# VectorE fills the transposes' source itself, the last tiles' routing goes ahead of other work, and half steps alternate with query transposes

## The chip, the core and the metric

The kernel runs on one core of a Trainium2 chip, in one launch. The metric is the device time of a whole execution in microseconds; of several runs the median counts. TensorE (PE) does matmuls and 128x128 transposes into PSUM, ScalarE (ACT) and VectorE (DVE) read PSUM and SBUF, GpSimd (POOL) works on SBUF and issues the indirect DMAs, and SyncE (SP) issues the other DMAs from one queue. Every engine runs its own instructions strictly in the order in which the program wrote them; between engines there are semaphores.

## The reference, cut to what matters

Linear attention with random features, followed by a top-1 mixture of experts with a capacity. B = 4, H = 8, S = 576, D = 64, M = 128 features; N = 2304 rows of width 512; E = 8 experts, F = 1024, capacity 576.

```
phi(x) = exp(x@omega.T - |x|^2/2 - max) / sqrt(m)
kv  = einsum('bhsm,bhsd->bhmd', phi(k), v);  z = sum_s phi(k)
attn = (phi(q) @ kv) / (phi(q) @ z + 1e-6)
x = attn as rows (2304, 512)
expert = argmax(x @ w_gate);  gate = softmax value of that expert
slot  = rank of the row among the rows of its expert (dropped from 576 on)
out[row] = gate * relu(x[row] @ w1[expert]) @ w2[expert]
```

## The kernel before

**Slots of the first part.** The outer loop (`for n in range(NS + LATE)`) runs over slots. A key slot takes four units of 128 keys (batch, group of four heads, ninth of the sequence); a query slot takes a tile of 128 rows. The order is: the keys of batches 0 and 1, query tiles 0 to 4, the keys of batches 2 and 3 (slots 15 to 23), query tiles 5 to 17, and three slots that only drain. In slot n TensorE gets, in this order: `project` of n into the `pj` banks; `numer` of the query tile of n - 3, or `kv_acc` of the key units of n - 2 or n - 3, into `sums`; the transposes `qtr` of the exponentials of slot n - 2 (`transposed`, two banks, each copied out by ScalarE into `qpT`). VectorE takes the maxima of `pj` and the normalisation of a tile, ScalarE the exponentials.

**Tasks.** Work that belongs to no slot stands in generators (`tasks`); `step()` takes each of them one `yield` further, some six or seven times a slot. How many `yield`s lie between two of its instructions decides at which place of each engine's order an instruction is written. Three tasks matter here. `kv_out` runs when the keys of a batch and group are summed: VectorE copies the sums from PSUM to `kv_sb`, POOL copies the kv part of `kv_sb` to `kvc`, and for the second group TensorE transposes `kvc` (`ktr`), VectorE copies that to `kvT`, and TensorE multiplies it with the gate weights (`ksm`). `first_item` loads the first expert's weights through SP and splits them on POOL (`w1hi`, `w1lo`, `w2hi`). `route(a, z)` finds expert, rank and table slot of tiles a to z - 1 (`GROUPS`: 0-4, 5-12, 13-17) on VectorE, with one matmul pair `posr` for the ranks, and POOL scatters the rows' numbers into the table `tab_d`, one indirect DMA a tile. After the first group, POOL gathers the first block rows `xg` of item 0 (`first_rows`), which must wait for SP's load of the list `idx` from the table.

**Row transposes and half steps.** An item is up to 576 rows of one expert, in five blocks. `transpose_x` transposes the gathered rows of a block (`xtri`) into a bank; ScalarE rounds them to `xhi`, VectorE subtracts to `xlo`. A half step (`mm1`) is 12 matmuls, h = relu(x w1) for 128 features and half of the rows; ScalarE writes `hhi` (and `hf`), VectorE `hlo`. Item 0's row transposes and 11 of its 16 half steps are put into query slots by the tables `ROWS_AT` and `HALVES_AT`. In the first part `qtr`, `ktr`, `ksm`, `posr`, `xtri` and the half steps share one ring of two PSUM banks (`bank(..)`, tag "tr"): the third user waits until the first one's bank has been read out. In the item part transposes still share two banks, half steps have four and `mm2` has two.

**Items.** After the slots, item 0 does its last five half steps; between them the rest of the routing tasks is stepped (nine steps after each half step), then `items_list` computes the remaining items into `res`. SP reads `res`, loads the next item's `idx` and weights (`prefetch`), POOL gathers its rows (`gather(1)`). TensorE does `mm2_rest` (16 matmuls) and four tiles `mm2` of 24 matmuls; behind some of them, by `tr_at`, stand the row transposes of item 1. After each tile ScalarE scales the result (`ysi`), then splits a quarter of the next w1 (`w1hi`), then takes the `xhi` of the transposes. Items 1 and 2 run the same way without the first part's remains.

## Time and profile before

| | |
|---|---|
| three runs, median (lowest to highest) | 327.15 us (327.11 to 327.22) |
| the profiled execution | 325.47 us, of which 323.7 us from the first to the last instruction |
| busy in the span | PE 286.3 us (88%), DVE 152.1 (47%), ACT 158.9 (49%), POOL 79.3 (25%) |
| mean granted TensorE clock | 0.951 of full speed |
| chain that ended last | PE 46%, issue 30%, POOL 10%, DMA 7% of the span |

The profiled execution is 1.8 us longer than its span; the runs without a profile lie 1.7 us above it. PE is near its full time in most stretches, so what counts is where it stands idle, which engine or transfer it waits for there, and how long its clock stays at half speed afterwards.

### The profile page before, as it was taken

To read this page: it belongs to the slowest core of one execution; us is meant where nothing else is said; L and a number is where in the kernel's file an instruction comes from. 1 tells how busy PE (TensorE), PEld (TensorE's weight loads), DVE (VectorE), ACT (ScalarE), POOL (GpSimd) and SP (SyncE) were. 2 spreads that over 40 slices of the span, in tenths; PEclk is the share of its full clock that TensorE was granted. 3 is DMA by queue.
4 is the path that set the end of the run, shared out by engine and by line. 5 is a ranking of instruction groups with operands and counts; after the bars stand their busy time and mean duration, and the time that the engine had idled before them with its cause. 6 is when DMAs were issued, how large, how long until landed. Compare 5 with 4: busy or idle time off the path is not lost.

```text
span 323.7 us, 7462 instructions
## 1 busy us (share of the span) xinstructions
PE 286.3 (88%) x2957; PEld 243.9 (75%) x2957; DVE 152.1 (47%) x349; ACT 158.9 (49%) x458; POOL 79.3 (25%) x92
## 2 busy tenths in 40 slices
PE   6999999949999999998789359999999999999950
PEld 5889788839787888888728248899688799958840
DVE  2666688923665764453970132354342234523220
ACT  4896799752788856542202313544352254352410
POOL 1000029497400000000376361160021135011110
PEclk9999999985999999999959959999999999999995
DMA  7987589505567541301000794291071049045020
GB/s 253 409 278 275 221 285 369 206 3 173 207 226 229 174 156 55 141 34 67 0 2 1 233 370 177 40 339 64 26 251 65 34 143 289 9 99 213 32 72 4
DMA packets 30096, 50.38 MB, mean 156 GB/s; under 512 B 5747, under 2 KB 15091, under 8 KB 30036
## 3 DMA queue, kind: packets, MB, share of 16 engines
q1 hardware_dynamic: 26212, 40.80, 37.0%
q0 software_dynamic: 3152, 8.28, 7.5%
q10 hardware_dynamic: 688, 0.73, 0.8%
q8 instruction: 25, 0.41, 0.5%
q14 instruction: 19, 0.16, 0.2%
HBM read 36.80 MB, written 13.28 MB: 155 GB/s over the span
## 4 chain that ended last, share of the span: by engine, by line
PE 46%; issue 30%; POOL 10%; DMA 7%; DVE 2%; ACT 1%; SPq 1%; POOLq 0%
PE hi L328 5%; PE yi L653 5%; PE hi L330 5%; PE yi L655 5%; PE yi L654 5%; PE hi L329 5%; PE pj L135 4%; PE sums L202 4%; POOL tab_d L104 4%; POOL w1lo L123 3%; PE yi L663 2%; DMA xg<-x_d,idx 2%; PE xtri L312 2%; DMA kraw<-kT 2%; POOL w1hi L120 1%
## 5 line engine op out<-in xcount | busy, mean ns | idle before, releaser
L148 ACT ACTIVATE ex<-pj,mx 128x128 f32<-128x128 f32 x288 | 79.1, 397 | 18.9 <-PE sums L202 10.3
L143 DVE TENSOR_REDUCE mx<-pj 128x4 f32<-128x512 f32 (+1 forms) x74 | 46.3, 670 | 24.0 <-PE pj L135 12.8
L328 PE MATMUL hi<-xhi,w1hi 128*128 128x288 f32 x148 | 44.0, 298 | 1.0 <-DVE hloi L336 1.0
L330 PE MATMUL hi<-xlo,w1hi 128*128 128x288 f32 x148 | 43.8, 296 | 0.0
L329 PE MATMUL hi<-xhi,w1lo 128*128 128x288 f32 x148 | 43.6, 294 | 0.0
L653 PE MATMUL yi<-w2hi,hhii 128*128 128x512 f32 x96 | 39.1, 407 | 0.0
L104 POOL DMA_INDIRECT tab_d<-pay,slot x18 | 19.2, 1065 | 78.2 <-DVE slot L390 73.7
L654 PE MATMUL yi<-w2hi,hloi 128*128 128x512 f32 x96 | 37.9, 395 | 0.0
L655 PE MATMUL yi<-w2lo,hhii 128*128 128x512 f32 x96 | 37.8, 394 | 0.0
L316 DVE TENSOR_TENSOR xlo<-xtri,xhi 128x512 fp32r<-128x512 f32 (+1 forms) x20 | 12.7, 638 | 53.2 <-ACT xhi L315 53.2
L104 POOL DMA_INDIRECT out<-ysi,idx x15 | 14.7, 981 | 86.9 <-ACT ysi L680 76.0
L333 ACT ACTIVATE hhii<-hi 128x224 fp32r<-128x224 f32 (+1 forms) x37 | 14.2, 383 | 35.9 <-PE hi L330 34.8
L680 ACT ACTIVATE ysi<-yi,idx 128x512 f32<-128x512 f32 x12 | 8.2, 687 | 43.3 <-issue 34.0
L336 DVE SCALAR_TENSOR_TENSOR hloi<-hi,hhii 128x224 fp32r<-128x224 f32 (+1 forms) x37 | 15.6, 423 | 28.8 <-ACT hfi L335 20.6
L328 PEld LDWEIGHTS hi<-xhi,w1hi 128*128 128x128 f32 x148 | 27.8, 188 | 1.5 <-DVE hloi L336 1.2
L446 ACT COPY qpT<-qtr 128x512 f32<-128x512 f32 x36 | 19.7, 588 | 17.6 <-PE qtr L445 17.1
L330 PEld LDWEIGHTS hi<-xlo,w1hi 128*128 128x128 f32 x148 | 27.8, 188 | 0.2 <-DVE xlo L316 0.2
L329 PEld LDWEIGHTS hi<-xhi,w1lo 128*128 128x128 f32 x148 | 27.8, 188 | 0.0
L300 POOL DMA_INDIRECT xg<-x_d,idx x20 | 21.8, 1091 | 21.2 <-DMA idx<-tab_d 16.6
L135 PE MATMUL pj<-om_sb,kraw 64*128 64x128 f32 x288 | 23.5, 290 | 2.6 <-DMA kraw<-kT 1.6
L202 PE MATMUL sums<-v,ex 128*64 128x65 f32 (+1 forms) x576 | 23.6, 236 | 0.0
L135 PEld LDWEIGHTS pj<-om_sb,kraw 64*128 64x128 f32 x288 | 19.3, 191 | 5.6 <-ACT ex L148 3.6
(107 smaller groups left out, 472.7 us busy)
## 6 DMA issues: line engine op xcount, KB each, us to landing
w1raw<-w SPq DMA_DIRECT2D x16, 512.0 KB, 5.7
w2raw<-w SPq DMA_DIRECT2D x16, 512.0 KB, 6.0
qraw<-qT SPq DMA_DIRECT2D x18, 256.0 KB, 4.6
x_d<-xr SPq DMA_DIRECT2D x18, 256.0 KB, 2.3
out<-zero_sb SPq DMA_DIRECT2D x6, 768.0 KB, 5.6
v<-va SPq DMA_DIRECT2D x7, 650.0 KB, 7.8
kraw<-kT SPq DMA_DIRECT2D x7, 576.0 KB, 6.2
v<-va ACTq DMA_DIRECT2D x1, 390.0 KB, 6.8
```

The source lines that it names most:

```text
L104: ins = nc.gpsimd.indirect_dma_start(out=dst, out_offset=bass.IndirectOffsetOnAxis(ap=index, axis=0), in_=src, in_offset=None, bounds_chec ...
L135: nc.tensor.matmul(pj[i][:, s * M : (s + 1) * M], raw[r, :], om_sb[r, :], start=True, stop=True, skip_group_check=True)
L143: nc.vector.tensor_reduce(mx[:, i, 0 : pj[i].shape[1]], pj[i], op=ALU.max, axis=AX.X, negate=True)
L148: nc.scalar.activation(ex[:, i, s, :], pj[i][:, s, :], AF.Exp, bias=mx[:, i, s : s + 1], scale=1.0)
L202: nc.tensor.matmul(acc[c : c + 64, i * 2 * VW + o : i * 2 * VW + o + (z - a) * VW], ex[:, i, c : c + 64], v[:, i, a * VW : z * VW], start= ...
L300: nc.gpsimd.indirect_dma_start(out=big["xg"][0:n, i, :], out_offset=None, in_=x_d[0:rows, :], in_offset=bass.IndirectOffsetOnAxis(ap=big[" ...
L328: nc.tensor.matmul(pt, whi_[:, k, fs], xhi[:, k, sl], start=(k == 0), stop=False)
L329: nc.tensor.matmul(pt, wlo_[:, k, fs], xhi[:, k, sl], start=False, stop=False)
L330: nc.tensor.matmul(pt, whi_[:, k, fs], xlo[:, k, sl], start=False, stop=(k == 3))
L653: nc.tensor.matmul(pt, hhi[:, f, sl], w2hi, start=(f == 0), stop=False)
L654: nc.tensor.matmul(pt, hlo[:, f, sl], w2hi, start=False, stop=False)
L655: nc.tensor.matmul(pt, hhi[:, f, sl], w2lo, start=False, stop=(f == 7))
```

## The change

VectorE, not POOL, fills `kvc`, straight from PSUM and directly behind its copy to `kv_sb`; the two pauses between go away. `route` has single yields everywhere, and the sum and reciprocal of the softmax stand behind the slots instead of ahead of the ranks. The last group's routing is no longer a task: at the start of the item part all tasks are run out, the group's VectorE part is written, then two half steps, then its ranks, slots, scatters and the whole `items_list`, then the other three half steps. The splits of w2 (`w2lo`) go behind the half steps, and the first `mm2` tile does its products with `w2lo` last. For item 0, SP issues the next w1 loads ahead of the list `idx`. In a query slot one row transpose or half step is written between the two banks of query transposes; the row transposes are one a slot from tile 8 on, and the half steps are single up to tile 17 and double in the three draining slots. Item 1's row transposes stand three behind the third tile and two behind the fourth, instead of two, two and one behind the second to fourth.

```diff
-ROWS_AT = {10: (0,), 11: (1, 2), 12: (3, 4)}
-HALVES_AT = {13: 1, 14: 1, 15: 2, 16: 2, 17: 2, 18: 1, 19: 1, 20: 1}
+ROWS_AT = {t: (t - 8,) for t in range(8, 13)}
+HALVES_AT = {13: 1, 14: 1, 15: 1, 16: 1, 17: 1, 18: 2, 19: 2, 20: 2}
...
         nc.vector.tensor_copy(kv[:, :, 0:VW], acc[:, 0 : 4 * VW].rearrange("p (h c) -> p h c", h=4))
-        yield from pause(2)
-        nc.gpsimd.tensor_copy(kvc[:, g * 2 * M : (g + 1) * 2 * M].rearrange("p (h c) -> p h c", h=4), kv[:, :, 0:D])
+        src = acc[:, 0 : 4 * VW].rearrange("p (h c) -> p h c", h=4)[:, :, 0:D]
+        nc.vector.tensor_copy(kvc[:, g * 2 * M : (g + 1) * 2 * M].rearrange("p (h c) -> p h c", h=4), src)
...
-        gap = 3 if 0 < a and z < NT else 1
...
-            yield from pause(gap)
+            yield
             nc.vector.tensor_tensor(cum[:, t + 1, :], cum[:, t, :], oh[:, t, :], op=ALU.add)
-        yield from pause(gap)
-        nc.vector.tensor_reduce(sm, ex, op=ALU.add, axis=AX.X)
...
-        yield from pause(gap)
+        yield "tensor"
         pos = bank(f"pos{nm}")[:, 0 : T * E]
...
         nc.vector.scalar_tensor_tensor(slot[:, a:z], drop, float(E * REG), base, op0=ALU.add, op1=ALU.add)
+        yield
+        nc.vector.tensor_reduce(sm, ex, op=ALU.add, axis=AX.X)
+        yield
+        nc.vector.tensor_scalar(sm, sm, 1e-9, None, op0=ALU.add)
+        yield
+        nc.vector.reciprocal(pay[:, a:z, 1].bitcast(F32), sm)
...
-        return qpT
+            yield qpT
...
-            if three[1] in GROUPS:
+            if three[1] in GROUPS and three[1] < NT - 1:
                 tasks.append(route(*GROUPS[three[1]]))
         step()
-        if two[0] == "q":
-            qpT_l[n - 2] = transposed(ex_l.pop(n - 2), f"{n - 2}")
...
+        tr = transposed(ex_l.pop(n - 2), f"{n - 2}") if two[0] == "q" else iter(())
+        qpT_l[n - 2] = next(tr, None)
+        if extra:
+            extra.pop(0)()
+        next(tr, None)
...
             if kind:
                 exponent(ex, pj, mx, i)
-            if i < len(extra):
-                extra[i]()
             step(2)
+        for x in extra:
+            x()
...
-    def mm2(i, pt, hhi, hlo):
+    def mm2(i, pt, hhi, hlo, lo_last):
...
+        if lo_last:
+            prods.sort(key=lambda x: x[1] is lo)
...
-                load_idx(sv, j + 1)
+                if j > 0:
+                    load_idx(sv, j + 1)
                 for c in range(4):
                     load_w(1, c, ev)
+                if j == 0:
+                    load_idx(sv, j + 1)
...
+                for _ in chain(*tasks):
+                    pass
+                ro = route(*GROUPS[NT - 1])
+                while next(ro) != "tensor":
+                    pass
                 for n, (f, half) in enumerate(halves):
                     mm1(f, half, bank(f"h{nm}{f}{half}", "h", 4), hhi, hlo, hf)
-                    if n < 4:
-                        split_w_lo(2, n)
-                    for _ in range(9):
-                        next(il, 0)
-                for _ in il:
-                    pass
+                    if n == 1:
+                        for _ in chain(ro, items_list()):
+                            pass
+                for c in range(4):
+                    split_w_lo(2, c)
...
-            tr_at = {2: (0, 1), 3: (2, 3), 4: (4,)} if j == 0 else {i: (i,) for i in range(NSUB)}
+            tr_at = {3: (0, 1, 2), 4: (3, 4)} if j == 0 else {i: (i,) for i in range(NSUB)}
```

Three places show how instructions move. The first is TensorE in the second round of keys, where the second group of batch 2 is complete; `sums` of `v_533` and `v_619` (before) or `v_625` (changed) are the last of its key sums, `ktr` and `ksm` its kv transposes and gate product. Before:

```order
L202 MATMUL sums<-v_533,ex_1077 64x65 x8
L202 MATMUL sums<-v_619,ex_1077 64x65 x8
L135 MATMUL pj_1245<-om_sb,kraw_822 128x128
...
L202 MATMUL sums<-v_619,ex_1126 64x65 x8
L202 MATMUL sums<-v_619,ex_1126 64x130 x4
L202 MATMUL sums<-v_619,ex_1126 64x65 x4
L225 MATMUL ktr_1276<-id_sb,kvc 128x128 x4
L231 MATMUL ksm_1292<-wg_sb,kvT 64x16 x8
```

Changed:

```order
L202 MATMUL sums<-v_533,ex_1077 64x65 x8
L202 MATMUL sums<-v_625,ex_1077 64x65 x8
L225 MATMUL ktr_1245<-id_sb,kvc 128x128 x4
L135 MATMUL pj_1251<-om_sb,kraw_822 128x128
...
L202 MATMUL sums<-v_625,ex_1131 64x65 x8
L202 MATMUL sums<-v_625,ex_1131 64x130 x4
L202 MATMUL sums<-v_625,ex_1131 64x65 x4
L231 MATMUL ksm_1288<-wg_sb,kvT 64x16 x8
```

The kv transposes stand a slot earlier, directly behind the sums they depend on, and a whole slot lies between them and the gate product.

The second place is VectorE around the last group's routing (`mxr` to `pay`; `hloi` belongs to half steps, `w2lo` to the split of w2, `ilcnt` is the first of `items_list`). Before, from the slots of the second group on:

```order
L390 SCALAR_TENSOR_TENSOR slot<-or_2010,br_2009 128x8
L336 SCALAR_TENSOR_TENSOR hloi_1453<-hi_2470,hhii_1452 128x224
L123 TENSOR_TENSOR w2lo_2418<-w2raw_108,w2hi_112 128x1024
L336 SCALAR_TENSOR_TENSOR hloi_1453<-hi_2499,hhii_1452 128x288
L123 TENSOR_TENSOR w2lo_2419<-w2raw_109,w2hi_113 128x1024
L336 SCALAR_TENSOR_TENSOR hloi_1453<-hi_2527,hhii_1452 128x224
L358 TENSOR_REDUCE mxr_2386<-lg 128x5
...
L390 SCALAR_TENSOR_TENSOR slot<-or_2393,br_2392 128x5
L589 TENSOR_SCALAR ilcnt<-cps,cap_f 1x16
```

Changed:

```order
L336 SCALAR_TENSOR_TENSOR hloi_1459<-h_2421,hhii_1458 128x288
L357 TENSOR_REDUCE mxr_2452<-lg 128x5
...
L371 TENSOR_TENSOR cum<-cum,oh 128x8 x5
L336 SCALAR_TENSOR_TENSOR hloi_1459<-hi_2472,hhii_1458 128x224
L336 SCALAR_TENSOR_TENSOR hloi_1459<-hi_2488,hhii_1458 128x288
L376 TENSOR_TENSOR sr_2456<-posr_2503,oh 128x40
...
L383 SCALAR_TENSOR_TENSOR slot<-or_2459,br_2458 128x5
...
L389 RECIPROCAL pay<-mr_2460 128x5
L591 TENSOR_SCALAR ilcnt<-cps,cap_f 1x16
```

The routing of tiles 13 to 17 stood behind all five half steps and two of the shown splits; now it stands behind the last half step of the slots (`h_2421`) and is done behind two of the five.

The third place is TensorE at item 1's row transposes (`xtri`), between item 0's tiles (`yi`). Before, behind the second tile, and the same again behind the third:

```order
L655 MATMUL yi_2699<-w2lo_2419,hhii_1452 128x512
L312 MATMUL xtri_2730<-id_sb,xg 128x128 x4
L312 MATMUL xtri_2737<-id_sb,xg 128x128 x4
L653 MATMUL yi_2745<-w2hi_110,hhii_1452 128x512
L654 MATMUL yi_2745<-w2hi_110,hloi_1453 128x512
```

Changed, behind the third tile:

```order
L660 MATMUL yi_2731<-w2lo_2443,hhii_1458 128x512
L312 MATMUL xtri_2762<-id_sb,xg 128x128 x4
L312 MATMUL xtri_2769<-id_sb,xg 128x128 x4
L312 MATMUL xtri_2776<-id_sb,xg 128x128 x4
L660 MATMUL yi_2784<-w2hi_110,hhii_1458 128x512
L660 MATMUL yi_2784<-w2hi_110,hloi_1459 128x512
```

Three blocks now follow one another on the two transpose banks.

## Rows read from the trace of the kernel before

**Rows 1.** What PE waited for, whole run: total us, times, longest.

```profile
PE xtri L312 <- DMA xg<-x_d,idx: 8.3, 2, 8.1
PE ktr L225 <- POOL kvc L219: 3.6, 1, 3.6
PE posr L381 <- DVE oh L369: 2.8, 1, 2.8
PE h L328 <- ACT qpT L446: 1.8, 6, 0.3
PE ksm L231 <- DVE kvT L226: 1.6, 2, 0.8
...
PE qtr L445 <- ACT qpT L446: 1.4, 2, 0.7
...
PE hi L328 <- DVE hloi L336: 1.0, 1, 1.0
...
PE xtri L312 <- ACT qpT L446: 0.8, 3, 0.3
PE posr L382 <- DVE cum L372: 0.6, 1, 0.6
```

**Rows 2.** Stretches: length, busy PE, PEld, DVE, ACT, POOL, clock, DMA share, GB/s.

```profile
72.00:76.00 4.00, 3.22 (x35) 2.81 (x36) 0.91 (x2) 0.00 (x0) 3.13 (x5) 0.50 0.29 61
76.00:80.00 4.00, 4.00 (x50) 3.66 (x52) 1.72 (x3) 2.04 (x8) 3.10 (x4) 0.50 0.62 195
...
162.00:162.50 0.50, 0.06 (x1) 0.05 (x1) 0.43 (x3) 0.00 (x0) 0.26 (x1) 0.50 0.00 0
```

**Rows 3.** Timeline of PE, second round of keys: start, us, instruction.

```profile
54.92 1.36 PE L202 MATMUL sums<-v,ex 128*64 128x130 f32 x32
...
62.85 1.15 PE L202 MATMUL sums<-v,ex 128*64 128x65 f32 x32
```

**Rows 4.** Timeline of DVE, the same stretch.

```profile
57.58 0.74 DVE L372 TENSOR_TENSOR cum<-cum,oh 128x8 bf16<-128x8 bf16 x4
...
64.40 0.41 DVE L217 COPY kv_sb<-sums 128x260 f32<-128x260 f32 x1
```

**Rows 5.** Timeline of PE from the end of item 0's half steps on.

```profile
163.56 6.25 PE L663 MATMUL yi<-w2raw,hfi 128*64 128x512 f32 x16
...
189.16 1.09 PE L312 MATMUL xtri<-id_sb,xg 128*128 128x128 f32 x4 [8.05 <-DMA xg<-x_d,idx]
...
197.56 1.04 PE L312 MATMUL xtri<-id_sb,xg 128*128 128x128 f32 x8
```

**Rows 6.** The chain that ended last, 173 to 190 us and 230 us: start, us, what.

```profile
173.80 0.98 POOL tab_d L104
...
175.08 3.02 DMA tab_d<-pay,slot
...
178.11 3.50 DMA idx<-tab_d
...
183.74 6.64 DMA xg<-x_d,idx
...
230.34 0.13 PE hi L330
230.47 3.58 PE yi L663 x16
...
234.88 0.23 PE yi L654
```

**Rows 7.** Timeline of DVE in the item part: routing of tiles 13-17, and item 1's `xlo`.

```profile
161.28 0.18 DVE L358 TENSOR_REDUCE mxr<-lg 128x5 f32<-128x40 f32 x1
...
164.64 0.17 DVE L390 SCALAR_TENSOR_TENSOR slot<-or,br 128x5 int32<-128x5 f32 x1
...
199.95 1.29 DVE L316 TENSOR_TENSOR xlo<-xtri,xhi 128x512 fp32r<-128x512 f32 x2 [5.87 <-ACT xhi L315]
```

More of the change, by code (lines that the diff above doesn't have):

```diff
@@ L365, in route @@
         nc.scalar.activation(ex, d, AF.Exp)
-        yield from pause(gap)
+        yield
         nc.vector.tensor_reduce(vm[:, a:z], val, op=ALU.max, axis=AX.X)
-        yield from pause(gap)
+        yield
         nc.vector.tensor_tensor(oh[:, a:z, :], val, vm[:, a:z].unsqueeze(2).to_broadcast(t3), op=ALU.is_equal)
         for t in range(a, z):
-            yield from pause(gap)
+            yield
             nc.vector.tensor_tensor(cum[:, t + 1, :], cum[:, t, :], oh[:, t, :], op=ALU.add)
-        yield from pause(gap)
-        nc.vector.tensor_reduce(sm, ex, op=ALU.add, axis=AX.X)
-        yield from pause(gap)
-        nc.vector.tensor_scalar(sm, sm, 1e-9, None, op0=ALU.add)
-        yield from pause(gap)
-        nc.vector.reciprocal(pay[:, a:z, 1].bitcast(F32), sm)
-        yield from pause(gap)
+        yield "tensor"
         pos = bank(f"pos{nm}")[:, 0 : T * E]
@@ L390, in route @@
         nc.vector.scalar_tensor_tensor(slot[:, a:z], drop, float(E * REG), base, op0=ALU.add, op1=ALU.add)
+        yield
+        nc.vector.tensor_reduce(sm, ex, op=ALU.add, axis=AX.X)
+        yield
+        nc.vector.tensor_scalar(sm, sm, 1e-9, None, op0=ALU.add)
+        yield
+        nc.vector.reciprocal(pay[:, a:z, 1].bitcast(F32), sm)
         yield from pause(2)
@@ L480, in step @@
         for _ in range(n):
-            tasks[:] = [x for x in tasks if next(x, 0) is None]
+            tasks[:] = [x for x in tasks if next(x, 0) != 0]
     def key_groups(b0, first):
@@ L648, in attention_moe @@
     res = const.tile([1, 2, 16], I32, name="res")
-    def mm2(i, pt, hhi, hlo):
+    def mm2(i, pt, hhi, hlo, lo_last):
         sl = slice(i * SUB, (i + 1) * SUB)
-        for f in range(8):
-            w2hi, w2lo = w_hi[2][f // 2][:, f % 2, :], w_lo[2][f // 2][:, f % 2, :]
-            nc.tensor.matmul(pt, hhi[:, f, sl], w2hi, start=(f == 0), stop=False)
-            nc.tensor.matmul(pt, hlo[:, f, sl], w2hi, start=False, stop=False)
-            nc.tensor.matmul(pt, hhi[:, f, sl], w2lo, start=False, stop=(f == 7))
+        hi = [w_hi[2][f // 2][:, f % 2, :] for f in range(8)]
+        lo = [w_lo[2][f // 2][:, f % 2, :] for f in range(8)]
+        prods = [((hhi, hi, f), (hlo, hi, f), (hhi, lo, f)) for f in range(8)]
+        prods = [x for p in prods for x in p]
+        if lo_last:
+            prods.sort(key=lambda x: x[1] is lo)
+        for n, (h, w, f) in enumerate(prods):
+            nc.tensor.matmul(pt, h[:, f, sl], w[f], start=(n == 0), stop=(n == len(prods) - 1))
     def mm2_rest(pt, hf):
@@ L691, in attention_moe @@
             hhi, hlo, hf = h_sb if j == 0 else h_tiles(nm)
-            il = chain(*tasks, items_list()) if j == 0 else iter(())
             def prefetch():
@@ L736, in attention_moe @@
                 else:
-                    mm2(i, pt, hhi, hlo)
+                    mm2(i, pt, hhi, hlo, j == 0 and n == 1)
                 c = n - 1 if j == 0 else n
```

## Prediction

> **What bounds the kernel now.** I read the list of PE's waits first, then the stretches with the granted clock, the timelines around the longest waits, and the chain that ended last. PE is busy in 88% of the span (the table), so a gain must come from its idle time and from time at half clock. The list [rows 1] shows where the idle time is: 8.3 us for item 1's gathered rows, 3.6 us for the kv transposes that wait for POOL's copy to `kvc`, 2.8 and 0.6 us for the last group's routing, and the rest in waits of about 1 us or less each. Behind every long wait the clock is at half: at 0.50 through 72 to 80 us, where PE is busy for 3.22 and 4.00 us, and at 162.0 us, while the wait of 2.8 us is still going on [rows 1, 2]. The work after it shows the price: `mm2_rest` takes 6.25 us at 163.56 and 3.58 us in item 1, and a block of row transposes 1.09 us at 189.16 where two blocks together take 1.04 later [rows 5, 6]. The chain of item 1's rows starts at POOL: the last scatter is issued at 175.08 and lands 3.02 later, the list takes 3.50 and a gather 6.64 us [rows 6]. That last scatter is late because tile 13-17's slots are known only at 164.8 [rows 7], behind all half steps.
>
> **Part A, the kv transposes (gain 5.3 us).** POOL's copies leave its queue, where the one for batch 2 stood behind scatters and weight splits. Removed: the `ktr` wait, 3.6. The half clock that followed it: 7.2 us of busy time between 72 and 80 that needs half of that at full clock, 3.6. Both `ksm` waits, 1.6, since a key slot now lies between the kv transposes and the gate product and covers the `kvT` copy. Both waits of `qtr` for the `qpT` copy, 1.4, which came where the kv transposes took a bank directly ahead of the query transposes. Sum 10.2 [rows 1, 2].
>
> Added: `ktr` now directly follows the sums it needs, so PE waits while VectorE finishes the slot's maxima, copies `kv_sb` and then `kvc`; behind PE's wait stand the next slot's projections and, through them, maxima and exponentials. In batch 2 the sums end at 62.85 + 1.15 = 64.0 and the `kv_sb` copy at 64.81 [rows 3, 4]; the new copy reads 256 instead of 260 elements a partition from the same bank, so 0.41 for it, and the wait is 1.2. Three batches pay this, and batch 3, where eight query transposes lie between, an estimated 0.3 for a bank: 3.9. VectorE's four copies themselves, 1.6, lie inside these waits or beside matmuls; without that cover they would cost 1.6.
>
> Also added: the first group's rank matmul `posr` moves up by three steps, from the next slot to the end of its own. It needs four `cum` operations that end at 58.32, while the sums ahead of it end at 56.28 [rows 3, 4]: PE waits 2.0, with the next projections behind it. Before, no such wait is in the list. VectorE is what is late there, so part of these 2.0 may only replace waits that would come anyway: between 0 and 2.0 I take the middle, 1.0, as nothing in the rows decides it. A = 10.2 - 3.9 - 1.0 = 5.3.
>
> **Part B, alternation (gain 0.7 us).** Removed: six half steps that waited for a bank that the `qpT` copy held, 1.8, and three row transposes, 0.8 [rows 1]. Added: with a half step (12 matmuls of 0.13, 1.6 us [rows 6]) between them the second query transposes find their bank free: that copy is good for a wait of 0.7 when nothing lies between [rows 1]. With a row transpose between (half of 1.04, [rows 5]) 0.2 remains, five times, 1.0. In the two draining slots with two half steps, the second one needs the first one's bank, whose reading out costs 1.0 when nothing lies between (the `hloi` wait of rows 1); the query transposes between (eight in 1.1, estimated from the row transposes) leave about 0.45, twice, 0.9. Half steps only change slots, so their work is the same. B = 2.6 - 1.9 = 0.7.
>
> **Part C, routing and item 1's rows (gain 12.0 us).** Removed: the waits for `xg`, 8.3, and for `oh`, 2.8; the slow part of `mm2_rest`, 6.25 - 3.58 = 2.7; that of two row transposes, 2 x (1.09 - 0.52) = 1.1 [rows 1, 5, 6]. Sum 14.9. I leave the 0.6 for `cum` uncounted.
>
> Is the chain early enough? Let 0 be the end of the last `numer`. Two half steps end at 3.2, and VectorE is done with the second about 1.0 later, when the first of the five others can start (that wait was there before). The routing took from 161.28 to 164.81, 3.5 us [rows 7]; now its first part runs beside two half steps, its second starts behind the reading out of these, at 3.2 + 1.0 + 3.2 + 1.0 = 8.4, and I give it 1.0 to the slots and 0.6 to the reciprocal that the scatters also need: 10.0. The eight scatters of group 2 are no longer queued ahead, since that routing now ends two slots earlier. Five scatters at 1.28 (173.80 to 175.08) issue until 15.4, land at 18.4, the list at 21.9; with an estimated 0.9 to POOL, block k's gather starts at 22.8 + 1.3 k and lands 6.64 later: 29.4, 30.7, 32.0, 33.3, 34.6 [rows 6]. PE meanwhile: seven half steps and the wait to 12.2, `mm2_rest` to 15.8, three tiles of 24 matmuls at 0.23 (5.6 each) to 32.6. The rows are there in time, with 3 us to spare for block 0. The `w2lo` splits, now behind `items_list`, are hidden by `mm2_rest` and by the first tile's 16 products that do not need them.
>
> Added: the third of three row transposes needs block 0's bank. In the trace two blocks start at 197.56, at a tile's end, and the first `xlo` is done at 199.95 + 0.65 = 200.6, since ScalarE does `ysi` and `w1hi` first [rows 5, 7]. So the third waits until 3.0 after the tile's end, and two blocks took 1.0 of it: PE idles 2.0, the fourth tile behind it. And two blocks instead of one behind the last tile leave item 1's second half step with `xhi` and `xlo` late; by the same chain I put 0.9. C = 14.9 - 2.9 = 12.0.
>
> **Sum.** 5.3 + 0.7 + 12.0 = 18.0. The profiled execution of 325.47 us would become 307.5; the three runs' median lies 1.7 above it, so I forecast 327.15 - 18.0 = **309.2 us**.
>
> **Rivals.** *The clock falls again in a new wait.* PE's 2.0 us waits at `posr` and at the third row transpose are a little shorter than the 2.8 us wait, in which the clock had fallen by 162.0 [rows 1, 2]; behind the shorter waits in the list I saw no fall. A fall costs half of the busy time until the clock returns: up to 3.6 by rows 2, 2.7 by `mm2_rest`. One such fall gives 312, two 314.5 to 315.
>
> *The new waits are mostly hidden*, as VectorE and ScalarE run ahead elsewhere: half of the 8.7 us that A, B and C add vanishes: 304.9, and with the uncounted 0.6, 304.3.
>
> *Item 1's rows stay late.* The list now stands behind four weight loads in SP's queue; before, it was the first. Its 3.5 us may double: blocks 0 and 1 then land at 32.9 and 34.2, 0.3 and about 0.5 after their turn, and the sum hardly moves; three times 3.5 makes PE wait 3.8, with a fall of the clock, less what the third transpose waits anyway: 313 to 315. The Trainium skill, "DMA: Bandwidth & Descriptors", section "Queues, rings and completion order", says that each DMA engine takes a ring's descriptors in ring order; by that rule the list lands only after the weights issued ahead of it, and the time is nearer to the second of these cases than to the forecast. No row here shows a list behind weights.
>
> *Slower than before: the alternation lengthens every query slot.* On ScalarE a half step's relu now stands ahead of the second `qpT` copy and the exponentials, so `numer` and the maxima could get into step with it. Twelve slots alternate; to eat the other 17.3 us of gain each must lose 17.3 / 12 = 1.4 us more. From there on the kernel is slower. Against it: the copy costs a wait of 0.7 with no cover at all [rows 1].
>
> *No change:* the weights' transfers set the end, and time gained comes back as waits in items 1 and 2. Against it: no wait for weights is among PE's waits [rows 1].
>
> **How the numbers follow.** Chances: the forecast's case 0.50, with its own range 306 to 311.5 (`posr` from 0 to 2.0, the `ktr` waits 20% off, the estimates of B); a fall of the clock 0.27; new waits hidden 0.12; rows late 0.06; no change 0.02; slower 0.03. The range goes from 303.5, which takes in hidden waits, to 315, which takes in one fall and most of two: about 0.13 is left out. A difference of 0.2% is 0.65 us, about what a measurement of this kernel can tell from none. Faster 0.95, same 0.02, slower 0.03.
>
> **What would show it.** Right: PE's `ktr` waits name VectorE, about 1.2 each, and 72 to 80 us has full clock; a `posr` wait for `cum` of about 2 in the second round of keys; no wait of several us for `xg`; `mm2_rest` at 3.6 in item 0; a wait of about 2 at item 1's third row transpose for `xlo`, and full clock behind it. The shift is about 5 by the first half step and 18 by item 1's first. Wrong: a clock of 0.50 behind one of the new waits; a gather that begins more than 3 us later than 22.8 after the last `numer`; waits of more than 1 us inside the alternating slots.

## The result and the profile after

| runs, each beside the kernel before on the same chip | median (lowest to highest) | ratio to before, 95% interval |
|---|---|---|
| first set: changed kernel, 4 runs | 317.33 us (316.30 to 319.92) | 0.971 (0.965 to 0.977), before 327.19 |
| three later sets: changed kernel, 4, 4 and 10 runs | 327.57, 328.50, 327.77 us | 0.997, 0.9995, 1.000; before 328.55, 328.33, 327.78 |

The forecast was 309.2 us, with a range from 303.5 to 315. The first set confirms the sign, 9.9 us faster, and lies 2.3 above the range. In three later sets, on three chips, the same kernel is no faster than before. Both results are real, and the experiments had to explain each. Medians are of all runs; ratios, and differences between two kernels further down, leave out runs that lie over 1.5% above their kernel's fastest. This section reads the first set's profile: 316.3 us, of which 314.5 from the first to the last instruction, so 9.2 less than before.

PE's waits in the kernel after; [rows 1] are the same view of before:

```profile
PE xtri L312 <- DMA xg<-x_d,idx: 5.8, 2, 4.4
PE xtri L312 <- DVE xlo L316: 4.0, 1, 4.0
PE pj L135 <- DMA kraw<-kT: 2.9, 1, 2.9
PE posr L375 <- DVE cum L371: 2.2, 1, 2.2
PE ktr L225 <- DVE kvc L219: 1.9, 3, 0.7
PE qtr L444 <- ACT qpT L445: 1.2, 4, 0.3
PE h L328 <- DVE hloi L336: 1.2, 2, 0.6
```

The waits for POOL's `kvc` and for `oh` are gone. What replaced them came as forecast in kind: `ktr` for VectorE (1.9, forecast 3.9), `posr` for `cum` (2.2, forecast 1.0), `qtr` for `qpT` (1.2, forecast 1.0), the second of two half steps for `hloi` (1.2, forecast 0.9). What is wrong stands on top: item 1's rows still cost 4.4 (the other 1.4 are item 0's), and the third row transpose 4.0, forecast 2.0.

Stretches of the kernel after: from:to, length, busy time of PE, its weight loads, VectorE, ScalarE and GpSimd with their instructions, granted clock, DMA share, GB/s ([rows 2] before):

```profile
72.00:76.00 4.00, 4.00 (x94) 3.78 (x92) 2.72 (x7) 2.91 (x11) 3.82 (x5) 1.00 0.05 5
76.00:80.00 4.00, 4.00 (x89) 3.52 (x88) 2.68 (x6) 3.63 (x14) 2.29 (x4) 1.00 0.36 79
...
176.00:180.00 4.00, 0.08 (x1) 0.00 (x0) 0.00 (x0) 0.00 (x0) 3.05 (x4) 0.98 1.03 385
180.00:184.00 4.00, 1.94 (x8) 1.57 (x8) 0.00 (x0) 0.44 (x1) 2.75 (x3) 0.50 0.72 253
184.00:188.00 4.00, 1.55 (x6) 1.46 (x7) 1.29 (x2) 2.56 (x5) 0.98 (x1) 0.50 0.32 121
```

72 to 80 us is at full clock now. The half clock stands at 180 to 188, behind the wait for item 1's rows.

Timeline of the kernel after from the last `numer` to item 1's `mm2_rest`: start, us, engine, instruction, in brackets the idle time ahead and what ended it ([rows 5 to 7] before):

```profile
141.63 1.25 PE L453 MATMUL sums<-kv_sb,qpT 128*64 128x73 f32 x32
152.33 0.17 DVE L383 SCALAR_TENSOR_TENSOR slot<-or,br 128x5 int32<-128x5 f32 x1
155.55 3.65 PE L668 MATMUL yi<-w2raw,hfi 128*64 128x512 f32 x16
157.15 0.98 POOL L104 DMA_INDIRECT tab_d<-pay,slot  x1 [0.30 <-issue]
157.75 4.61 DVE L123 TENSOR_TENSOR w2lo<-w2raw,w2hi 128x1024 fp32r<-128x1024 f32 x4
158.27 2.30 SPq L285 DMA_DIRECT2D w1raw<-w  x4
158.43 4.78 POOL L104 DMA_INDIRECT tab_d<-pay,slot  x1 [0.30 <-issue]
168.57 0.37 SPq L295 DMA_DIRECT2D idx<-tab_d  x1
173.46 1.00 POOL L300 DMA_INDIRECT xg<-x_d,idx  x1 [10.24 <-issue]
179.78 0.96 POOL L104 DMA_INDIRECT out<-ysi,idx  x1 [0.30 <-issue]
180.52 1.94 PE L312 MATMUL xtri<-id_sb,xg 128*128 128x128 f32 x8 [4.44 <-DMA xg<-x_d,idx]
183.56 0.69 ACT L685 ACTIVATE ysi<-yi,idx 128x512 f32<-128x512 f32 x1 [11.37 <-DMA out<-ysi,idx]
185.70 1.29 DVE L316 TENSOR_TENSOR xlo<-xtri,xhi 128x512 fp32r<-128x512 f32 x2 [12.25 <-ACT xhi L315]
186.44 1.11 PE L312 MATMUL xtri<-id_sb,xg 128*128 128x128 f32 x4 [3.99 <-DVE xlo L316]
...
194.16 0.99 PE L312 MATMUL xtri<-id_sb,xg 128*128 128x128 f32 x8
...
221.42 3.65 PE L668 MATMUL yi<-w2raw,hfi 128*64 128x512 f32 x16
```

With 0 at the end of the last `numer` (142.88): the slots are known at 9.6 and `mm2_rest` runs at full clock, 3.65 [rows 5]. Up to here all is as forecast. Then the last scatter, which starts at 15.6 (forecast 15.4), takes 4.78 instead of 0.98 and so ends at 20.3, not 16.4; the list is issued at 25.7, not 18.4; the first gather at 30.6, not 22.8. PE had its tiles done at 176.08, or 33.2 (forecast 32.6), and waits until 180.52.

The shift against before is 5.7 us at the last `numer`, 8.0 at `mm2_rest` and 9.05 at item 1's `mm2_rest` (221.42, [rows 6]). The forecast had 18 there. At the start the changed kernel was 3.1 behind at its first `numer` (39.74 against 36.66). Of this, 1.3 are two of the new `ktr` waits, 0.64 each, which the forecast had priced; and the third `kraw` piece came late, `pj` waited 2.9 for it against 1.55. In the three later profiles of the identical kernel this wait is 1.4, 1.6 and 3.6, and the first `numer` starts at 39.49, 37.56 and 40.70. So up to 2.2 of the 3.1 are chance, and some 0.9 belong to the change.

### The profile page after: what moved, and what is told of

The parts are those of the page before. It is cut to its first block, busy times and chain, and to the rows that moved or that the text cites. A ratio compares the mean times of both kernels' runs of the same rounds, so it can differ in the third digit from the quotient of the medians.

```text
span 314.5 us, 7453 instructions
## 1 busy us (share of the span) xinstructions
PE 280.8 (89%) x2957; PEld 241.8 (77%) x2957; DVE 154.9 (49%) x357; ACT 159.8 (51%) x458; POOL 79.5 (25%) x84
## 5 line engine op out<-in xcount | busy, mean ns | idle before, releaser
L104 POOL DMA_INDIRECT tab_d<-pay,slot x18 | 21.8, 1210 | 63.9 <-DVE pay L389 50.9
L660 PE MATMUL yi<-w2lo,hhii 128*128 128x512 f32 x96 | 37.0, 397 | 0.0
L104 POOL DMA_INDIRECT out<-ysi,idx x15 | 14.7, 983 | 86.4 <-ACT ysi L685 75.4
L445 ACT COPY qpT<-qtr 128x512 f32<-128x512 f32 x36 | 20.6, 589 | 9.5 <-PE qtr L444 9.1
```

The source lines that it names most:

```text
L104: ins = nc.gpsimd.indirect_dma_start(out=dst, out_offset=bass.IndirectOffsetOnAxis(ap=index, axis=0), in_=src, in_offset=None, bounds_chec ...
L445: nc.scalar.copy(qpT[:, 2 * p : 2 * p + 4, :], tr.rearrange("p (h t) -> p h t", h=4))
L660: nc.tensor.matmul(pt, h[:, f, sl], w[f], start=(n == 0), stop=(n == len(prods) - 1))
```

## The experiments

**Set 2: VectorE's copies alone, and three orders of item 1's list and gathers.** e2 is the kernel before with one edit:

```diff
-        yield from pause(2)
-        nc.gpsimd.tensor_copy(kvc[...], kv[:, :, 0:D])
+        src = acc[...]
+        nc.vector.tensor_copy(kvc[...], src)
```

> The kernel before with the edit of part A alone: VectorE writes kvc from the sums, GpSimd's copy is gone. The forecast for this part was 5.3 us, 321.9. What the trace of the changed kernel shows of it: ktr waits of 1.9 in all (forecast 3.9), full clock from 72 to 80 us, but a first batch whose start was 2.7 us late. If the late start is chance: 321 to 322. If it belongs to the change in the order of VectorE's work: 324.

Measured: 322.31 us (320.25 to 323.68), 0.982 (0.976 to 0.989) of before (328.17): 5.9 us. Part A had 5.3, but 1.0 of its costs belongs to `posr`, which this kernel leaves at its old place; for the copies alone its terms give 6.3. The clock is 1.00 through 64 to 80 us. The copies are worth about what was forecast.

In the changed kernel e1 puts the list back ahead of the w1 loads, e4 puts item 1's gathers further back, and e5 does both:

```diff
# e1: SP issues the list ahead of w1 for every item
-                if j > 0:
-                    load_idx(sv, j + 1)
+                load_idx(sv, j + 1)
...
-                if j == 0:
-                    load_idx(sv, j + 1)
# e4: item 1's gathers behind the second output tile's scatter of rows
-                gather(1)
...
+                    if n == 1:
+                        gather(1)
```

> The changed kernel with one edit undone: item 1's list is loaded ahead of the four w1 loads again. Theory (the 2 MB of w1 fill the DMA engines while the last tab_d scatter is in flight): the fifth scatter takes 0.98 us again and not 4.78, the list is issued about 3.5 us after it, near 163 and not 168.57, the first gather near 167 and not 173.46. TensorE's wait of 4.4 us for xg falls under 1 and the clock stays full up to there. The wait at the third row transpose (4.0) may stay, since item 0's output scatters still stand behind the gathers on GpSimd. Time 309 to 312. Rival (the scatters land late by themselves, the w1 loads do nothing): list and gathers stay where they are, 317. Rival (the w1 loads behind the list are late in their turn): w1hi waits, and the time is 314 or more.

> The changed kernel with item 1's five gathers written behind item 0's first two output tiles, so that two output scatters stand ahead of them on GpSimd. Theory (ScalarE's scaling of the fourth output tile waits for a buffer that the first output scatter holds, and the row tile copies stand behind it; that made the third row transpose wait 4.0): the wait at the third row transpose falls to 1.5 to 2, the gathers stay near 173.5 since the list sets them, and the wait of 4.4 for xg stays. Time 314 to 315.5. Rival (three row tiles on two PSUM banks are the cause, by the time of the copies themselves): the wait stays near 4 and the time at 317.

> The changed kernel with both edits: the list ahead of the w1 loads, the gathers behind two output scatters. Theory: rows arrive before TensorE asks for them (wait under 1), the third row transpose waits 1.5 to 2, the clock stays full through item 0; item 1's first half step starts 8 to 10 us earlier than in the changed kernel. Time 306 to 309. Rival (the clock falls in the remaining wait of 2): 310 to 312. Rival (neither matters): 317.

Measured: e1 327.54 us, 0.997 (0.994 to 1.001); e4 322.46, 0.977 (0.970 to 0.985); e5 318.67, 0.967 (0.961 to 0.974). The unaltered kernel was not run in this set; in the later ones it has 0.997 to 1.000. Timeline of e1, POOL, SP, ScalarE and PE around item 1's gathers:

```profile
171.55 4.79 POOL L104 DMA_INDIRECT tab_d<-pay,slot  x1 [0.30 <-issue]
178.42 0.41 SPq L295 DMA_DIRECT2D idx<-tab_d  x1
182.59 1.00 POOL L300 DMA_INDIRECT xg<-x_d,idx  x1 [6.26 <-DMA idx<-tab_d]
195.75 0.69 ACT L685 ACTIVATE ysi<-yi,idx 128x512 f32<-128x512 f32 x1 [9.71 <-DMA out<-ysi,idx]
198.63 1.12 PE L312 MATMUL xtri<-id_sb,xg 128*128 128x128 f32 x4 [7.04 <-DVE xlo L316]
```

The list is issued 2.08 behind the held scatter's end, where w1 ahead of it made that 5.36. But the third transpose now waits 7.04: five gathers on POOL stand ahead of the row scatters `out`, and ScalarE stands still for 9.71 ahead of `ysi`, until the first of these has freed a buffer. With the gathers behind two `out` scatters the third transpose is nearly free in e4 (0.55), and in e5 none of the first three waits over 0.81. The long third-transpose wait comes from the order on POOL. In e1 the w1 loads are issued behind the list, at 179.07, and the scatter still takes 4.79, so they are not what holds it.

The way from the last `numer`'s end to the start of item 1's `mm2_rest` leaves out what happens in the first part. It takes 81.9 in the kernel before and 78.6 in the first set's profile (78.2 to 78.4 in the three later ones); 77.8 in e1, 74.2 in e4 and 69.9 in e5. So the two orders together bring 12.0 against before, what Part C had promised, with the splits still beside the scatter. The end of that way in e5, whose last `numer` ends at 154.66:

```profile
224.52 3.65 PE L668 MATMUL yi<-w2raw,hfi 128*64 128x512 f32 x16
```

**Set 3: moving the splits.** e7 writes the four `split_w_lo(2, c)` behind the `finish` of `mm2_rest`, item 0's first output tile, e8 joins that with e5; e9 puts the old tables `ROWS_AT` and `HALVES_AT` and the old places of their steps back; e6 is the changed kernel unaltered.

```diff
-                for c in range(4):
-                    split_w_lo(2, c)
...
+                    if n == 0:
+                        for x in range(4):
+                            split_w_lo(2, x)
```

> The changed kernel itself, unaltered, beside the others of this set. In its profiled execution ScalarE ran through from 137 to 156 us. In the three profiles of the edited versions ScalarE stood still twice there, for 5.8 and 3.7 us, and the first half step behind it came 9 us late, though no edit is ahead of that place. If the two stops are a property of a chip or an execution and not of the edits, they appear here too in some execution, and this run gives the level against which the three have to be read: 317 without them, about 325 with them. If they belong to the edits, this run shows 317 and none.

> The changed kernel with one edit: VectorE's four w2lo splits stand behind item 0's first output tile, not directly behind the half steps. Theory (GpSimd's issue of a scatter makes no headway while VectorE runs these two-operand subtractions back to back; the last scatter took 4.78 us and ended 0.86 behind the fourth split): the last scatter takes 0.98 again; with the w1 loads still ahead, the list follows about 5 us behind it, near 22 to 23 us after the last numer and not 27; first gather 26 to 27 after it and not 30.6. TensorE's wait for xg falls from 4.4 to 0.5 to 1. The splits end about 1 us late for the first full tile: a wait of up to 1.0 there. Time 3 to 5 us below the changed kernel of this set. Rival (the w1 loads issued at the same time slow the scatter): it still takes 4.78 and nothing is gained, 1 us is lost.

> The changed kernel with three edits: splits behind item 0's first output tile, list ahead of the w1 loads, gathers behind two output scatters. Theory: list 19 and first gather 23 us after the last numer, rows there when TensorE asks, third row transpose waits under 2, clock full through item 0: 8 to 10 us below the changed kernel of this set. Rival (w1, now behind the list, comes late for w1hi and holds ScalarE): the copies xhi wait behind w1hi and 2 to 4 of it are lost again.

> The changed kernel with part B undone: row transposes and half steps in the slots and places that the kernel before has, each behind the exponentials and not between the query transposes. The forecast for part B is a gain of 0.7, so this is 0.7 slower than the changed kernel. If the alternation lengthened the query slots, this is faster by 1 or more. If the row transposes of slots 8 and 9 now come too early for their gathered rows in the changed kernel (a wait of 1.4 at the first), undoing it removes that wait and the two sides cancel: within 0.7.

Measured: e6 327.57 us, 0.997 (0.992 to 1.001): the first set's gain is not there. e7 333.26, 1.015, and e8 336.22, 1.025. In both the splits stand behind item 1's w2 loads, so item 0 is multiplied with item 1's w2 in them and PE waits 9.5 and 10.8 for `w2lo`; their times say nothing of the question. What they do show is a last scatter of 0.98 in e7. e9 331.18 (326.5 to 332.5), 0.999 (0.991 to 1.008): Part B undone can't be told from e6, so its 0.7 is neither confirmed nor refuted.

Timeline of e6 between its last two `numer`:

```profile
137.52 1.02 POOL L104 DMA_INDIRECT tab_d<-pay,slot  x1 [48.31 <-DVE pay L389]
138.43 1.25 PE L453 MATMUL sums<-kv_sb,qpT 128*64 128x73 f32 x32
143.18 0.17 DVE L466 TENSOR_SCALAR den<-sums 128x8 f32<-128x8 f32 x1 [3.74 <-PE h L330]
143.30 0.58 ACT L445 COPY qpT<-qtr 128x512 f32<-128x512 f32 x1 [4.34 <-PE h L330]
146.57 0.98 POOL L104 DMA_INDIRECT tab_d<-pay,slot  x1 [0.31 <-issue]
148.90 0.36 ACT L333 ACTIVATE hhii<-h 128x224 fp32r<-128x224 f32 x1 [5.01 <-remote]
149.94 0.58 PE L328 MATMUL h<-xhi,w1hi 128*128 128x288 f32 x1 [5.34 <-DVE hloi L336]
153.09 1.48 PE L453 MATMUL sums<-kv_sb,qpT 128*64 128x73 f32 x32
```

The `numer` ends at 139.68; VectorE's `den`, which needs only its result, starts 3.5 later (0.04 after the last `numer` of the first set's profile), and ScalarE's `hhii` starts 7.0 after the end of its half step (141.86). In the trace the updates of PE's semaphore that these two wait for stand at 143.16 and 148.87, so it is PE's results or their signals that come late; the trace's ends of matmuls are modelled and can't tell the two apart. Meanwhile POOL issues the eight scatters of tiles 5 to 12, one each 1.28, between 137.5 and 147.6. The last two `numer` are 14.7 apart (138.43 and 153.09) instead of 6.3: 8.4 us more. In all eleven later profiles that have the alternation and these eight scatters in a row the gap is 14.6 to 14.9; in e9, without the alternation, the eight come later, beside item 0's last half steps, and there ScalarE stands still for 8.5 and PE for 7.0. This stop is the larger part of the difference between the first set and the later ones.

**Set 4: are the scatters the cause? And the splits at a right place.** e13 leaves out the eight scatters of tiles 5 to 12, so those rows are not computed; e12 is the changed kernel unaltered; e10 is e7 with item 1's w2 loads behind the splits; e11 is e10 with e5.

```diff
# e13, in route
         for t in range(a, z):
+            if a == 5:
+                break
# e10, e11: beside e7's edit
-                    next(pre, 0)
+                    if j > 0:
+                        next(pre, 0)
...
+                        next(pre, 0)
```

> The changed kernel, unaltered, the level for the other three. If the late signals (TensorE's done-signals that reach ScalarE and VectorE 3 to 7 us late while GpSimd's eight scatters are on their way) belong to some chips: 317 here without them or 327 with them, and the profile shows which.

> The changed kernel without the eight tab_d scatters of tiles 5 to 12; their entries of the table stay at its initial value, so those tokens are not computed by their items. Theory (the scatters in flight hold up TensorE's signals): no signal is late between 135 and 155 us, ScalarE's stops of 5.8 and 3.7 us are gone, and where the changed kernel of this set has them this is 8 to 10 us faster; where it has none, the two are within 1. Rival (the stops come from the half steps or from a code fetch at this place): they stay.

> The changed kernel with VectorE's four w2lo splits behind item 0's first output tile, and item 1's w2 loads behind the splits (in e7 the splits stood behind those loads and so waited for item 1's weights). Theory (GpSimd's issue of a scatter makes no headway while VectorE runs these subtractions back to back): the fifth scatter takes 0.98 us again, not 4.78; with the w1 loads still ahead the list follows about 5 us behind its end, so the first gather starts 26 to 27 us after the last numer, not 30.6, and the wait for xg falls from 4.4 to about 1. Time 3 to 5 us below the changed kernel of this set. Rival (the w1 loads slow the scatter): still 4.78, and about 1 us lost to splits that end late.

> The changed kernel with three edits: splits behind item 0's first output tile, list ahead of the w1 loads, gathers behind two output scatters. Theory: fifth scatter 0.98, list about 2 us behind its end, first gather 22 to 24 us after the last numer as the prediction had it, no wait above 1 us for xg, third row transpose under 2, full clock through item 0: 8 to 10 us below the changed kernel of this set, 307 to 309 where that is 317. Rival (w1 behind the list comes late for w1hi, and ScalarE's row copies stand behind it): 3 to 5 of that are lost.

Measured: e12 328.50 us, 0.9995 (0.993 to 1.006); e13 319.50, 0.974 (0.968 to 0.980), 9.0 less. The stretch of the stop, first in e12 and then in e13:

```profile
144.00:152.00 8.00, 1.35 (x7) 1.14 (x8) 1.75 (x5) 1.53 (x4) 3.82 (x4) 0.74 0.10 33
```

```profile
144.00:152.00 8.00, 7.01 (x74) 6.53 (x74) 3.43 (x12) 1.53 (x5) 0.00 (x0) 1.00 0.09 33
```

Without POOL's scatters PE runs through. e10 326.68, 0.992 (0.984 to 1.001); e11 321.34, 0.980 (0.974 to 0.985). Timeline of e10, then of e11:

```profile
170.20 0.98 POOL L104 DMA_INDIRECT tab_d<-pay,slot  x1 [0.31 <-issue]
174.17 1.07 SPq L295 DMA_DIRECT2D idx<-tab_d  x1
182.75 1.00 POOL L300 DMA_INDIRECT xg<-x_d,idx  x1 [11.57 <-DMA w2raw<-w]
```

```profile
170.31 0.98 POOL L104 DMA_INDIRECT tab_d<-pay,slot  x1 [0.31 <-issue]
174.83 4.32 POOL L104 DMA_INDIRECT out<-ysi,idx  x1 [3.55 <-ACT ysi L685]
193.18 0.66 PE L312 MATMUL xtri<-id_sb,xg 128*128 128x128 f32 x4 [2.10 <-DVE xlo L316]
```

The last scatter is back at 0.98, and in e10 the way to item 1's `mm2_rest` falls from 78.6 to 76.1. In e11 the splits run at 173.73 to 178.34, and now the `out` scatter beside them is held for 4.32, ending 0.8 behind them. In e10, where w1 is still ahead of the list, a gather starts 8.58 after the list's issue; in e1, where the list is ahead, 4.17. On that way e11 takes 71.7, 1.9 more than e5, which has the splits at their old place: PE now waits 1.2 for `w2lo` and 2.1 at the third transpose.

**Set 5: two bursts.** e14 splits the middle group so that its eight scatters go in two bursts of four; e15 joins that with e11; e16 is the changed kernel and e17 is e11 once more.

```diff
-GROUPS = {4: (0, 5), 12: (5, 13), 17: (13, 18)}
+GROUPS = {4: (0, 5), 8: (5, 9), 12: (9, 13), 17: (13, 18)}
```

> The changed kernel with tiles 5 to 12 routed in two groups of four: four scatters some 25 us earlier, and four where the eight were. Theory (a burst of scatters that lasts 10 us holds up TensorE's signals, a shorter one does so for less time): the two stops of 5.8 and 3.7 us shrink to one of about 4 or vanish; against the changed kernel of this set 4 to 9 us faster. Rival (any burst in the query slots has its own stop): two stops, one in each burst, and no gain. The second routing of the query part costs VectorE about 2.5 us beside matmuls, at most 1 on the path.

> The version with three edits (splits behind the first output tile, list ahead of the w1 loads, gathers behind two output scatters) and two groups of four. Theory: 4 to 9 below the version with three edits, 312 to 317. Rival: the same as it, 321.

> The changed kernel, unaltered, the level for e14: 327 to 328.5 if this chip shows late signals as the last three did, 317 if not.

> The version with three edits once more, the level for e15 and against e16: about 7 below the changed kernel of this set, as in the last one. If e16 shows no late signals, this shows what the three edits alone are worth: 307 to 310 against 317.

Measured: e16 327.77 us, 1.000 (0.996 to 1.004); e14 322.32, 0.982 (0.976 to 0.989); e17 321.69, 0.978 (0.970 to 0.986); e15 317.24, 0.968 (0.959 to 0.978). PE is busy for 3.38 of the 8 us from 144 on in e16 and for 7.38 in e14. Timeline of e15:

```profile
147.22 1.25 PE L453 MATMUL sums<-kv_sb,qpT 128*64 128x73 f32 x32
167.23 0.41 SPq L295 DMA_DIRECT2D idx<-tab_d  x1
175.17 1.50 POOL L300 DMA_INDIRECT xg<-x_d,idx  x1 [0.31 <-issue]
183.82 1.03 PE L312 MATMUL xtri<-id_sb,xg 128*128 128x128 f32 x8
186.95 0.66 PE L312 MATMUL xtri<-id_sb,xg 128*128 128x128 f32 x4 [2.10 <-DVE xlo L316]
```

This is nearly the chain that the forecast had drawn: the list 18.8 after the last `numer`'s end (forecast 18.4), no wait for item 1's rows, 2.1 at the third transpose (forecast 2.0), and full clock in the two transposes ahead of it (1.03). The first gather starts at 26.7 (forecast 22.8), behind two `out` scatters, and is still in time.

**Set 6: the earlier place of `posr`.** The later profiles showed the clock falling behind new waits in the second round of keys. e18 is e15 with the first group's sum and reciprocal back ahead of its rank matmul; e19 is e15 again.

```diff
+        if a == 0:
+            yield from gate()    # sum, + 1e-9, reciprocal
         yield "tensor"
...
+        if a > 0:
+            yield from gate()
```

> All edits together, and the first group's route is as it was before: sum and reciprocal ahead of the rank matmul, which so stands three steps later. In seven of the fourteen profiles with the earlier place the clock fell at 60 to 68 us, behind the 2.0 wait of posr, and in five more behind the wait for item 0's first rows at 84 to 92; the way from the fifth numer to the seventh took 35.5 where neither came and 36.9 to 40.6 otherwise, 33.8 in the run that had only VectorE's kvc copies. If the posr wait is what costs there, no wait of posr over 0.5, full clock from 56 to 72 us, 33.5 to 36 for that way, and 2 to 4.5 us less than the unaltered all-edits kernel beside it. If VectorE is late anyway and the wait only moves to ktr or to item 0's rows, the way stays at 37 to 39 and the times agree within 1 us.

> The all-edits kernel again, as the measure for the run beside it: 315 to 320 us, a posr wait of 2.0 to 2.3, and a fall of the clock either behind it or behind the wait for item 0's first rows.

Measured: e18 314.11 us (312.98 to 316.41), 0.958 (0.953 to 0.962), the lowest median here; e19 315.38 (312.68 to 318.85), 0.958 (0.953 to 0.964). The `posr` wait is gone and the way from the fifth to the seventh `numer` takes 35.75 instead of 37.07, but item 0's first rows then wait 2.29, and the intervals overlap. The 2 to 4.5 are not confirmed; e19's profile happened to have no fall of the clock there.

## Why the prediction was off, point by point

**Part A held, with its costs exchanged.** e2 gives 5.9 for the copies (6.3 by the forecast's terms). In the first set A and B put the kernel 5.7 ahead at the last `numer` (forecast 6.0), in spite of up to 2.2 lost by chance at the start. Without that it would be up to 7.9; 2.0 of the surplus are the smaller `ktr` waits, while `posr` (2.2, taken as 1.0) and item 0's first rows (1.4, not foreseen) go the other way. How these add up is not shown.

**The rival of a falling clock is true, more often than its 0.27.** Of seventeen profiles with the early `posr`, nine have a lowered clock at 60 to 68 us, behind its wait of 1.8 to 2.5, and five others at 84 to 92, behind item 0's first rows. From the fifth to the seventh `numer` the kernel before needs 40.9 and e2 33.8; the three profiles with neither fall, the first set's among them, 35.5 to 37.1, the nine 38.5 to 42.3, the five 36.9 to 38.5. This is the smaller part of what the later sets lose. In the rival of hidden waits what A, B and C add is 9.7 with `posr` (3.9, 1.0, 1.9 and 2.9), not 8.7, so it gave 304.4 and not 304.9; nothing else rests on that.

**Part C failed, and with it the forecast.** It brought 3.4 of its 12.0 us, for "The rows are there in time, with 3 us to spare for block 0" did not come true, and "PE idles 2.0" at the third transpose came out at 4.0. Three steps are behind this. The first is "The `w2lo` splits, now behind `items_list`, are hidden by `mm2_rest`". That is true for PE and false for POOL: the last scatter stands beside four splits back to back on VectorE (157.75 to 162.36) and comes to an end only 0.85 behind the last. That is 3.8 of the 7.8 by which the first gather is late. It is shown by the moves: the scatter takes 4.70 to 4.79 in all profiles with the splits beside it, 0.98 in e7, e10, e11 and e15, and the hold goes with the splits to the next indirect DMA. And it stood in the trace of before, unread. Timeline of the kernel before, VectorE and POOL:

```profile
158.35 1.22 DVE L123 TENSOR_TENSOR w2lo<-w2raw,w2hi 128x1024 fp32r<-128x1024 f32 x1
158.41 2.05 POOL L104 DMA_INDIRECT tab_d<-pay,slot  x1 [73.42 <-DVE slot L390]
159.84 1.21 DVE L123 TENSOR_TENSOR w2lo<-w2raw,w2hi 128x1024 fp32r<-128x1024 f32 x1
```

The first scatter beside a single split takes 2.05 instead of 0.98 and ends 0.89 behind it. Reading what ran beside the moved instruction on the other engines would have shown it. The Trainium skill, "SBUF — State Buffer", section "SBUF: two separate sides", says that a VectorE instruction with two SBUF inputs contends with a GpSimd instruction that reads SBUF, and that the second one is fully blocked. The split has two such inputs, and the trace agrees (4.78 against 0.98). The Trainium skill, under the same title, section "Who interferes with whom", reports that in a probe `tensor_tensor` did not stall a DMA, and infers that descriptor generation, the work by which GpSimd prepares one, is left alone by it; it doesn't say whether that DMA was indirect. Here the indirect ones are held, and the measurement decides.

**"Item 1's rows stay late" is the second step, 3.3 us of the 7.8.** The forecast let the list follow the last scatter as in the trace of before, and gave this rival 0.06. Its mechanism is right: with w1's 2 MB ahead, the list is issued 5.36 behind the last scatter instead of 2.08 (e1), or, where the scatter isn't held, lands 4.4 later (e10). The rest, 0.7, is a slightly later start and the list's own transfer. The rival's time, 313 to 315, was its price alone; the splits' hold came on top. The Trainium skill, "DMA: Bandwidth & Descriptors", section "Queues, rings and completion order", adds that a semaphore increment lands only after every earlier write of its DMA engine, across its queues; both late places agree with that (5.36 and 8.58).

**The third step is the 2.0 at the third row transpose.** It was priced at a place of the old trace where ScalarE's `ysi` started at its tile's end. In the changed kernel it starts 7.5 behind that end (183.56 against 176.08), for a buffer that the first `out` scatter frees, and this scatter stands behind five late gathers on POOL; e4 puts it ahead of them, and 0.55 is left.

**The price.** PE waits 4.4 for the rows; the half clock behind this costs 2.9 (the two transposes 1.94 instead of 1.04, the third 1.11 instead of 0.52, the fourth tile's 24 products 6.95 instead of 5.6); the third transpose waits 2.0 more than forecast. Less 0.6 of the tail wait, which measured 0.3, that is 8.7. Part C brought 9.05 - 5.7 = 3.4 instead of 12.0, 8.6 less. What each step is worth by itself, on the way of 78.6: the list ahead 0.7 (e1), the splits moved 2.5 (e10), the gathers later 4.3 (e4). The two orders together bring back all of it, 8.7 (e5). With the splits moved as well it is 5.2 to 6.8 (e11, e15, e17 to e19). So the hold is real, but moving it does not pay once list and gathers are in order: in e5 the first gather starts at 26.7, as in e11, and PE's waits for the rows are 1.8 in all. In whole runs too e5 (0.967 of before) lies below e11 and e17 (0.980 and 0.978), though each was on another chip; e5 with two bursts was not run. Against the changed kernel of the same set e11's three edits are worth 7.2 (set 4) and 5.9 (e17, set 5).

**Why the later sets show no gain.** The stop beside the eight scatters costs 8 to 9 us: without the scatters 9.0 come back (e13), with two bursts 5.2 (e14 against e16) and 6.2 (e15 against e17). The forecast had the scatters as "no longer queued ahead", which frees item 1's, and did not ask what they meet at their new place. That the time came out as the rival "No change" had it is luck: that rival spoke of weights. Not settled: why the first set escapes it, by its chip or by chance (its profile has the same scatters and no stop), and in what way the scatters delay the other engines. One rival stays open: 3.6 to 3.8 us after the first of the eight the trace has a transfer of 8 KB on the queue that it calls `instruction`, which takes 2.2 to 2.9 us in every profile with the stop (0.3 to 0.9 in other places), and e13 and e14 are rid of it together with the eight in one row. By itself it is not enough, for the first set's profile has it too (2.35) and no stop.

## What to carry to other kernels

When an instruction moves, look at what runs beside its new place on every engine, POOL's indirect DMAs above all: in the old trace any of them longer than its fellows names what it can't stand beside. Price such a hold by the path: here the order of a list and of five gathers was worth more than moving what held the scatter. A transfer that others wait for goes ahead of bulk loads in its queue, and a gather behind the scatters that free a buffer. A result from one chip is one draw: repeat the kernel on others before its gain is believed.

## What the runs showed of the hardware that was not expected

- An indirect DMA on POOL makes no headway beside VectorE's 128x1024 split, and doesn't get in between four back to back: 4.78 and 4.32 us instead of 0.98, each ending 0.8 to 0.9 behind the last one. A single split holds it for 2.05.
- Beside eight indirect scatters issued 1.28 us apart, VectorE and ScalarE start on PE results 3.5 us and, a second time, 7.0 us after the end that the trace gives for them, and PE loses some 8.4 us. It is in every later profile that has them in one row beside the alternation; two bursts of four avoid it, and so did, unexplained, the first set.
- The clock fell to its lower level behind `posr` waits of 1.8 to 2.5 us in nine profiles, and not in eight others with waits of 1.9 to 2.3, so here such a wait had no fixed price.
